# Converting float64 weights 1024 values a partition at a time instead of twice 512

## The chip, the cores and the metric

One core of a Trainium2 chip runs the whole program. The metric is the device time in microseconds (us); lower is better. Engines are named as in the profile: PE (matrix engine), PEld (its weight loads), DVE (VectorE), ACT (ScalarE), POOL (GpSimd), SP (the queue that issues the DMA transfers).

## The reference

Three stages on 4608 tokens (8 batches of 576): pooled attention in float32, then two feed-forward layers. All weights of the layers are float64.

```python
def _attn_ref(q, k, v):                    # (8, 8, 576, 64), pool = 8
    k_p = k.reshape(B, H, Sp, pool, D).mean(axis=3)
    v_p = v.reshape(B, H, Sp, pool, D).mean(axis=3)
    scores = scale * np.matmul(q, k_p.transpose(0, 1, 3, 2))
    ...
    return np.matmul(attn, v_p).astype(np.float32)

def _moe_ref(x, w1, w2, w3, w_out):        # 512 -> 1024 -> 512
    a = x @ w1
    b = x @ w2
    h = a * b @ w3
    return (h @ w_out).astype(np.float32)

def _moe2_ref(x, w_in, w_out):             # 512 -> 2048 -> 512
    h = x @ w_in
    g = np.maximum(h, 0.0) + np.log1p(np.exp(-np.abs(h)))
    return (g @ w_out).astype(np.float32)
```

## The kernel before

**Conversion jobs.** The chip's engines compute in float32, so the kernel turns the float64 weights into float32 itself, from their bits. A job takes 1024 float64 values a partition (1 MB in all). `load_raw` loads them in two transfers of 512 values a partition, each into a buffer of its own (`raw`, four buffers). `convert_steps` then works in steps, each for both halves one after the other: ACT scales the high word (L100); DVE clamps (L103) and shifts it (L105); DVE puts in the sign (L108); DVE puts in the low word's bits (L111). For w12, wi and wo2 the result is split further into two terms of reduced precision for the fast matmul mode: ACT rounds it (L115) and DVE takes the remainder (L118). The intermediate tiles `y` of such a job come from the shared tag `t2k` (eight buffers). The steps of a job are a generator; `bg(n)` runs n steps of the queued jobs at a given place of the program, so conversions are scattered between other work. When a job ends, `load_ahead` issues the next load, so that two jobs' data are loaded or under way.

**Stages.** There are 36 jobs. First come twelve for the two matrices whose product W = w3 @ w_out replaces two of the reference's matmuls (names `wo`, `w3_`; their tiles are `wgh`/`wgl`); PE multiplies them (`W_mm`, tiles `Wp`) while the attention of the first token groups runs in slots between. `W_split` (ACT, then DVE, tiles `Wh`, `Wl`) ends that stage, and the first layer's matmuls (`ab`) follow. Eight jobs give the groups of w1 and w2 (`w_0` to `w_7`), three of them before W's split and five after it. From then on nine blocks of 512 tokens go through the first layer: a step multiplies x with a group of w1 (`ab`, even groups) and one of w2 (odd groups), DVE multiplies the two (`g`), ACT and DVE split the result (`gh`, `gl`), and a step later PE multiplies it with W (`x2p`). Two PSUM banks take turns for `ab`: the one that DVE's `g` reads is written again by the next step's second product. Attention slots lie between until all token groups are done. During the last two blocks the sixteen jobs of the second layer begin (`wi0` to `wi7`, and eight for wo2, tiles `w2h`, `w2l`): four are queued behind the last attention slot, 2 + 3 + 2 in the last block, and five for the first steps of the second layer. The second layer then runs 9 x 16 steps (`h`, softplus on ACT and DVE, `o`), the `o` product three steps behind `h`.

Between the layers x2 goes through DRAM; `x2_load` brings a block back, and `x2_split` splits its four parts.

**Order.** The program is written in order by hand; each engine runs its instructions in that order, and waits where one isn't ready. SP issues the transfers in that order too, and waits for the buffer of each.

Of the kernel before, what the change touches and what calls it, by code (L numbers as in the profile page):

```python
# [15 lines left out]
P = 128  # L16
# [32 lines left out]
def pooled_attention_two_ffn(ctx: ExitStack, tc: tile.TileContext, qT_d, kT_d, v_d, w12_d, w3T_d, wo_d, wi_d, wo2_d, out):  # L49
# [23 lines left out]
    def t2k(name, dt=F32):  # L73
        return main.tile([P, 512], dt, tag="t2k", name=name, bufs=8)
# [12 lines left out]
    def load_raw(src, name):  # L87

        raw = main.tile([P, 512, 2], I32, tag="raw", name=f"raw_{name}", bufs=4)
        nc.sync.dma_start(raw.rearrange("p n t -> p (n t)"), src.bitcast(I32))  # L90
        return raw

    def convert_steps(raws, dsts, name):


        both = range(len(raws))
        y = [t2k(f"y_{name}_{i}") if isinstance(dsts[i], tuple) else dsts[i] for i in both]
        yi = [t.bitcast(I32) for t in y]
        for i in both:
            nc.scalar.activation(y[i], raws[i][:, :, 1].bitcast(F32), AF.Abs, scale=HI_SCALE)  # L100
        yield
        for i in both:
            nc.vector.tensor_scalar(y[i], y[i], HI_MIN, HI_MAX, op0=ALU.max, op1=ALU.min)  # L103
        for i in both:
            nc.vector.tensor_scalar(yi[i], yi[i], 3, None, op0=ALU.logical_shift_left)  # L105
        yield
        for i in both:
            nc.vector.scalar_tensor_tensor(yi[i], raws[i][:, :, 1], -0x80000000, yi[i], op0=ALU.bitwise_and, op1=ALU.bitwise_or)  # L108
        yield
        for i in both:  # L110
            nc.vector.scalar_tensor_tensor(yi[i], raws[i][:, :, 0], 29, yi[i], op0=ALU.logical_shift_right, op1=ALU.bitwise_or)  # L111
        yield
        if isinstance(dsts[0], tuple):
            for i in both:
                nc.scalar.activation(dsts[i][0], y[i], AF.Copy)  # L115
            yield
            for i in both:
                nc.vector.tensor_sub(dsts[i][1], y[i], dsts[i][0].bitcast(F32))  # L118

# [7 lines left out]
    def load_ahead():  # L127
        while jobs and len(loaded) < 2:
            name, srcs, dst = jobs.pop(0)
            loaded.append((name, [load_raw(s_, f"{name}_{i}") for i, s_ in enumerate(srcs)], dst))  # L130

    def next_job():
        load_ahead()
        name, raws, dst = loaded[0]
        yield from convert_steps(raws, dst(), name)
        loaded.pop(0)
        converted.add(name)
        load_ahead()
# [11 lines left out]
    def add_group(src, slot, name, into):  # L150


        def dst():
            hi = main.tile([P, KD, 256], F32R, tag=f"wgh{slot}", name=f"{name}h")
            lo = main.tile([P, KD, 256], F32R, tag=f"wgl{slot}", name=f"{name}l")
            into[slot] = hi, lo
            return [tuple(w[:, 2 * i:2 * i + 2, :].rearrange("p k f -> p (k f)") for w in (hi, lo)) for i in range(2)]

        add_job(name, [src[:, 2 * i:2 * i + 2, :] for i in range(2)], dst)
# [8 lines left out]
    def load_q(n):  # L168
        t = ap_.tile([P, 4, 256], F32, tag="q", name=f"q{n}", bufs=3)
        nc.sync.dma_start(t, qT_d[n])  # L170
        q_t[n] = t
# [128 lines left out]
    for g in range(NG):  # L300
        o = STEPS_FIRST if g < 4 else STEPS_DENSE if g < 8 or g >= NG - 4 else STEPS
        if o[3] < o[4]:
            at(begin[g] + o[4], lambda g=g: x_split(g))
        at(begin[g], lambda g=g: scores(g))
        at(begin[g] + o[0], lambda g=g: softmax(g))
        at(begin[g] + o[1], lambda g=g: normalize(g))
        at(begin[g] + o[2], lambda g=g: p_transpose(g))
        at(begin[g] + o[3], lambda g=g: pv(g))
        if o[3] == o[4]:
            at(begin[g] + o[3], lambda g=g: x_split(g))  # L310
        if g % 2 == 1 and g // 2 + 3 < NG // 2:
            at(begin[g] + 1, lambda g=g: load_q(g // 2 + 3))
# [20 lines left out]
    with tc.manual_schedule():  # L333
# [13 lines left out]
        def wo_dst(kk):  # L347
# [5 lines left out]
            return [wo_hl[kk], wo_hl[kk + 1]]  # L353

        def w3_dst(kk):
            if kk % 2 == 0:
                w3_hl["t"] = tiles_of(4 + kk // 2, 512)
            w3_hl[kk] = w3_hl["t"][kk % 2]
            return [w3_hl[kk][:, 0, :], w3_hl[kk][:, 1, :]]

        for kk in range(K1):
            if kk % 2 == 0:
                add_job(f"wo{kk}", [wo_d[(kk + i) * P:(kk + i + 1) * P, :] for i in range(2)], lambda kk=kk: wo_dst(kk))
            add_job(f"w3_{kk}", [w3T_d[kk * P:(kk + 1) * P, 512 * i:512 * i + 512] for i in range(2)], lambda kk=kk: w3_dst(kk))
# [27 lines left out]
        for n in range(3):  # L392
# [4 lines left out]
            if n:  # L397
# [99 lines left out]
        def x2_load(j):  # L497
            raw = fin.tile([P, KD, TB], F32, tag="x2raw", name=f"x2r{j}")
            nc.sync.dma_start(raw, x2d[j])
            x2h[j, "raw"] = raw  # L500

        def x2_split(j, kk):
# [3 lines left out]
            split(x2h[j][:, kk, :], x2l[j][:, kk, :], x2h[j, "raw"][:, kk, :])  # L506
# [10 lines left out]
        x2_load(0)  # L517
        for i in range(K1):
            p1_step(NB - 1, i, [slot_3, slot_2, slot_2])
            if 1 <= i < 5:  # L520
                x2_split(0, i - 1)
            if i % 2 == 1 and i < 7:
# [64 lines left out]
        for n in range(len(seq) + LAG):  # L587
            if n < len(seq):
# [5 lines left out]
                if j + 1 < NB:  # L594
                    if f == 1:
                        x2_load(j + 1)
                    if f in (7, 9, 11, 13):
                        x2_split(j + 1, (f - 7) // 2)
# [55 lines left out]
```

## Time and profile before

| | |
|---|---|
| median of 3 runs | 1596.8 us (1596.24 to 1597.06) |
| profiled execution: its own time | 1598.61 us |
| profiled execution: span, first to last instruction | 1596.8 us |
| mean granted clock of PE | 0.996 of full speed |
| busy share of the span: PE, PEld, DVE, ACT | 97%, 79%, 53%, 50% |
| instructions: DVE, ACT | 1452, 1813 |
| DMA, mean | 60 GB/s |

The busy share is an average over stages. A time in a view counts from the span's start. PE's busy time holds matmuls whose ends are modelled. "Idle before" is the engine's idle time just ahead of an instruction, with what ended it.

### The profile page before, as it was taken

To read this page: it belongs to the slowest core of one execution; us is meant where nothing else is said; L and a number is where in the kernel's file an instruction comes from. 1 tells how busy PE (TensorE), PEld (TensorE's weight loads), DVE (VectorE), ACT (ScalarE), POOL (GpSimd) and SP (SyncE) were. 2 spreads that over 40 slices of the span, in tenths; PEclk is the share of its full clock that TensorE was granted. 3 is DMA by queue.
4 is the path that set the end of the run, shared out by engine and by line. 5 is a ranking of instruction groups with operands and counts; after the bars stand their busy time and mean duration, and the time that the engine had idled before them with its cause. 6 is when DMAs were issued, how large, how long until landed. Compare 5 with 4: busy or idle time off the path is not lost.

```text
span 1596.8 us, 19269 instructions
## 1 busy us (share of the span) xinstructions
PE 1556.2 (97%) x7424; PEld 1254.9 (79%) x7424; DVE 853.7 (53%) x1452; ACT 799.7 (50%) x1813; POOL 1.7 (0%) x8
## 2 busy tenths in 40 slices
PE   4898999999999999999999999999999999999999
PEld 2457888888888888878878888888888888888887
DVE  6896534243433434327878755555555555555554
ACT  3555433343434343334467665556565565565554
POOL 0000000000000000000000000000000000000000
PEclk9999999999999999999999999999999999999999
DMA  8652212021212111204341101000000001010000
GB/s 275 212 185 76 90 46 66 25 76 37 77 36 63 52 62 29 79 1 158 132 132 54 53 1 53 1 27 27 27 27 27 27 1 53 1 53 1 7 20 27
DMA packets 32011, 95.61 MB, mean 60 GB/s; under 512 B 3632, under 2 KB 3632, under 8 KB 30768
## 3 DMA queue, kind: packets, MB, share of 16 engines
q1 hardware_dynamic: 31920, 94.39, 18.1%
q8 instruction: 58, 0.95, 0.3%
q14 instruction: 33, 0.27, 0.1%
HBM read 75.50 MB, written 18.87 MB: 59 GB/s over the span
## 4 chain that ended last, share of the span: by engine, by line
PE 84%; DVE 8%; ACT 4%; DMA 2%; issue 1%; SPq 0%; ACTq 0%; DVEq 0%
PE ab L82 8%; PE o L573 7%; PE ab L84 7%; PE ab L83 7%; PE o L575 7%; PE o L574 7%; PE h L82 7%; PE h L83 7%; PE h L84 7%; PE x2p L82 4%; PE x2p L84 4%; PE x2p L83 4%; PE sc L213 2%; PE pv L262 2%; PE pTp L244 2%; DMA raw_w<-in_w3T_dram 1%
## 5 line engine op out<-in xcount | busy, mean ns | idle before, releaser
L79 DVE TENSOR_TENSOR g2l<-d,g2h 128x512 fp32r<-128x512 f32 x144 | 99.6, 692 | 328.9 <-ACT g2h L78 328.9
L573 PE MATMUL o<-w2h,g2h 128*128 128x512 f32 x576 | 224.8, 390 | 1.8 <-DVE x2s L445 1.7
L575 PE MATMUL o<-w2h,g2l 128*128 128x512 f32 x576 | 224.2, 389 | 0.0
L574 PE MATMUL o<-w2l,g2h 128*128 128x512 f32 x576 | 224.2, 389 | 0.0
L543 ACT ACTIVATE e<-h 128x512 f32<-128x512 f32 x144 | 85.8, 596 | 270.2 <-PE h L84 270.2
L78 ACT ACTIVATE gh<-g 128x512 fp32r<-128x512 f32 x72 | 45.5, 633 | 179.1 <-DVE g L428 179.1
L573 PEld LDWEIGHTS o<-w2h,g2h 128*128 128x128 f32 x576 | 108.1, 188 | 26.6 <-DVE x2s L445 2.1
L575 PEld LDWEIGHTS o<-w2h,g2l 128*128 128x128 f32 x576 | 108.1, 188 | 23.0 <-DVE g2l L79 0.4
L574 PEld LDWEIGHTS o<-w2l,g2h 128*128 128x128 f32 x576 | 108.1, 188 | 21.8
L82 PE MATMUL x2p<-gh,Wh 128*128 128x512 f32 x288 | 116.1, 403 | 0.0
L84 PE MATMUL x2p<-gh,Wl 128*128 128x512 f32 x288 | 112.6, 391 | 0.0
L83 PE MATMUL x2p<-gl,Wh 128*128 128x512 f32 x288 | 112.3, 390 | 0.0
L227 ACT ACTIVATE pr<-sc,mx 128x72 f32<-128x72 f32 x288 | 87.7, 331 | 48.8 <-DVE mx L225 48.7
L428 DVE TENSOR_TENSOR g<-a,ab 128x512 f32<-128x512 f32 x72 | 49.4, 686 | 108.1 <-PE ab L84 107.0
L553 DVE TENSOR_TENSOR d<-d,l 128x512 f32<-128x512 f32 x144 | 99.7, 692 | 5.0
L552 DVE SCALAR_TENSOR_TENSOR d<-h,d 128x512 f32<-128x512 f32 x144 | 99.6, 692 | 5.0
L551 DVE SCALAR_TENSOR_TENSOR d<-u,e 128x512 f32<-128x512 f32 x144 | 98.7, 685 | 1.0 <-ACT u L546 1.0
L79 DVE TENSOR_TENSOR xl<-pv,xh 128x512 fp32r<-128x512 f32 x36 | 24.8, 690 | 135.5 <-ACT xh L78 135.5
L546 ACT ACTIVATE u<-e 128x512 f32<-128x512 f32 x144 | 91.0, 632 | 10.1 <-DVE d L551 5.7
L548 ACT ACTIVATE l<-u 128x512 f32<-128x512 f32 x144 | 91.1, 633 | 4.7
L544 ACT ACTIVATE e<-e 128x512 f32<-128x512 f32 x144 | 91.0, 632 | 4.6
L78 ACT ACTIVATE g2h<-d 128x512 fp32r<-128x512 f32 x144 | 88.6, 615 | 3.5 <-DVE d L553 2.8
(207 smaller groups left out, 3209.7 us busy)
## 6 DMA issues: line engine op xcount, KB each, us to landing
raw_wo<-in_wo_dram SPq DMA_DIRECT2D x24, 512.0 KB
kv<-in_kT_dram SPq DMA_DIRECT2D x32, 288.0 KB
q<-in_qT_dram SPq DMA_DIRECT2D x18, 512.0 KB
kv<-in_v_dram SPq DMA_DIRECT2D x32, 288.0 KB
x2d<-x2s SPq DMA_DIRECT2D x36, 256.0 KB
x2r<-x2d SPq DMA_DIRECT2D x9, 1024.0 KB
out_dram<-os SPq DMA_DIRECT2D x36, 256.0 KB
raw_w<-in_w3T_dram SPq DMA_DIRECT2D x16, 512.0 KB
```

The lines of the kernel that those rows point to most:

```text
L78: nc.scalar.activation(hi, src, AF.Copy)
L79: nc.vector.tensor_sub(lo, src, hi.bitcast(F32))
L82: nc.tensor.matmul(ps, whi, xhi, start=first, stop=False)
L83: nc.tensor.matmul(ps, whi, xlo, start=False, stop=False)
L84: nc.tensor.matmul(ps, wlo, xhi, start=False, stop=last)
L548: nc.scalar.activation(ln, u, AF.Ln)
L551: nc.vector.scalar_tensor_tensor(d, u, 1.0, e, op0=ALU.subtract, op1=ALU.subtract)
L552: nc.vector.scalar_tensor_tensor(d, ps, 0.0, d, op0=ALU.max, op1=ALU.subtract)
L553: nc.vector.tensor_add(d, d, ln)
L573: nc.tensor.matmul(oacc[j][t], hi[:, s_], wh, start=f == 0, stop=False)
L574: nc.tensor.matmul(oacc[j][t], hi[:, s_], wl, start=False, stop=False)
L575: nc.tensor.matmul(oacc[j][t], lo[:, s_], wh, start=False, stop=f == K2 - 1)
```

## The change

A job's data lie in one buffer of 1024 values a partition (`raw`, two buffers) and each step of a job is one instruction over 1024 values. Weights whose rows lie in one piece in DRAM are loaded in one transfer (w3, w12, wi); wo and wo2, whose two halves are different rows, in two. `y` gets buffers of its own (`y4k`, two of 4 KB a partition). For w12 and wi the two steps of the further split work on 1024 values as well; for wo2 they stay two instructions of 512. To make room, `t2k` has six buffers instead of eight and `q` two instead of three (so the third q tile is loaded later), and `x2_load` brings half a block at a time into a buffer of half the size, the second half behind the second split.

```diff
@@ -71,7 +71,7 @@
         return at_p.tile([P, 512], F32, tag="at", name=name)
 
     def t2k(name, dt=F32):
-        return main.tile([P, 512], dt, tag="t2k", name=name, bufs=8)
+        return main.tile([P, 512], dt, tag="t2k", name=name, bufs=6)
 
     def split(hi, lo, src):
 
@@ -84,39 +84,37 @@
         nc.tensor.matmul(ps, wlo, xhi, start=False, stop=last)
 
 
-    def load_raw(src, name):
-
-        raw = main.tile([P, 512, 2], I32, tag="raw", name=f"raw_{name}", bufs=4)
-        nc.sync.dma_start(raw.rearrange("p n t -> p (n t)"), src.bitcast(I32))
+    def load_raw(srcs, name):
+
+        raw = main.tile([P, 1024, 2], I32, tag="raw", name=f"raw_{name}", bufs=2)
+        n = 1024 // len(srcs)
+        for i, src in enumerate(srcs):
+            nc.sync.dma_start(raw[:, n * i:n * i + n, :].rearrange("p n t -> p (n t)"), src.bitcast(I32))
         return raw
 
-    def convert_steps(raws, dsts, name):
-
-
-        both = range(len(raws))
-        y = [t2k(f"y_{name}_{i}") if isinstance(dsts[i], tuple) else dsts[i] for i in both]
-        yi = [t.bitcast(I32) for t in y]
-        for i in both:
-            nc.scalar.activation(y[i], raws[i][:, :, 1].bitcast(F32), AF.Abs, scale=HI_SCALE)
+    def convert_steps(raw, dst, name):
+
+
+        split_ = isinstance(dst, list)
+        y = main.tile([P, 1024], F32, tag="y4k", name=f"y_{name}", bufs=2) if split_ else dst
+        yi = y.bitcast(I32)
+        nc.scalar.activation(y, raw[:, :, 1].bitcast(F32), AF.Abs, scale=HI_SCALE)
         yield
-        for i in both:
-            nc.vector.tensor_scalar(y[i], y[i], HI_MIN, HI_MAX, op0=ALU.max, op1=ALU.min)
-        for i in both:
-            nc.vector.tensor_scalar(yi[i], yi[i], 3, None, op0=ALU.logical_shift_left)
+        nc.vector.tensor_scalar(y, y, HI_MIN, HI_MAX, op0=ALU.max, op1=ALU.min)
+        nc.vector.tensor_scalar(yi, yi, 3, None, op0=ALU.logical_shift_left)
         yield
-        for i in both:
-            nc.vector.scalar_tensor_tensor(yi[i], raws[i][:, :, 1], -0x80000000, yi[i], op0=ALU.bitwise_and, op1=ALU.bitwise_or)
+        nc.vector.scalar_tensor_tensor(yi, raw[:, :, 1], -0x80000000, yi, op0=ALU.bitwise_and, op1=ALU.bitwise_or)
         yield
-        for i in both:
-            nc.vector.scalar_tensor_tensor(yi[i], raws[i][:, :, 0], 29, yi[i], op0=ALU.logical_shift_right, op1=ALU.bitwise_or)
+        nc.vector.scalar_tensor_tensor(yi, raw[:, :, 0], 29, yi, op0=ALU.logical_shift_right, op1=ALU.bitwise_or)
         yield
-        if isinstance(dsts[0], tuple):
-            for i in both:
-                nc.scalar.activation(dsts[i][0], y[i], AF.Copy)
+        if split_:
+            n = 1024 // len(dst)
+            parts = [y[:, n * i:n * i + n] for i in range(len(dst))]
+            for part, (hi, lo) in zip(parts, dst):
+                nc.scalar.activation(hi, part, AF.Copy)
             yield
-            for i in both:
-                nc.vector.tensor_sub(dsts[i][1], y[i], dsts[i][0].bitcast(F32))
-
+            for part, (hi, lo) in zip(parts, dst):
+                nc.vector.tensor_sub(lo, part, hi.bitcast(F32))
 
 
     jobs, loaded, converted = [], [], set()
@@ -127,12 +125,12 @@
     def load_ahead():
         while jobs and len(loaded) < 2:
             name, srcs, dst = jobs.pop(0)
-            loaded.append((name, [load_raw(s_, f"{name}_{i}") for i, s_ in enumerate(srcs)], dst))
+            loaded.append((name, load_raw(srcs, name), dst))
 
     def next_job():
         load_ahead()
-        name, raws, dst = loaded[0]
-        yield from convert_steps(raws, dst(), name)
+        name, raw, dst = loaded[0]
+        yield from convert_steps(raw, dst(), name)
         loaded.pop(0)
         converted.add(name)
         load_ahead()
@@ -154,9 +152,9 @@
             hi = main.tile([P, KD, 256], F32R, tag=f"wgh{slot}", name=f"{name}h")
             lo = main.tile([P, KD, 256], F32R, tag=f"wgl{slot}", name=f"{name}l")
             into[slot] = hi, lo
-            return [tuple(w[:, 2 * i:2 * i + 2, :].rearrange("p k f -> p (k f)") for w in (hi, lo)) for i in range(2)]
-
-        add_job(name, [src[:, 2 * i:2 * i + 2, :] for i in range(2)], dst)
+            return [tuple(w.rearrange("p k f -> p (k f)") for w in (hi, lo))]
+
+        add_job(name, [src.rearrange("p k f -> p (k f)")], dst)
 
 
     ident = main.tile([P, P], F32, tag="ident", name="ident")
@@ -166,7 +164,7 @@
     q_t, kT_t, vb_t, kv_raw = {}, {}, {}, {}
 
     def load_q(n):
-        t = ap_.tile([P, 4, 256], F32, tag="q", name=f"q{n}", bufs=3)
+        t = ap_.tile([P, 4, 256], F32, tag="q", name=f"q{n}", bufs=2)
         nc.sync.dma_start(t, qT_d[n])
         q_t[n] = t
 
@@ -308,8 +306,8 @@
         at(begin[g] + o[3], lambda g=g: pv(g))
         if o[3] == o[4]:
             at(begin[g] + o[3], lambda g=g: x_split(g))
-        if g % 2 == 1 and g // 2 + 3 < NG // 2:
-            at(begin[g] + 1, lambda g=g: load_q(g // 2 + 3))
+        if g % 2 == 1 and g // 2 + 2 < NG // 2:
+            at(begin[g] + 1, lambda g=g: load_q(g // 2 + 2))
 
 
     first, last = {}, {}
@@ -350,18 +348,18 @@
             t = wo_hl["t"][kk // 2 % 2]
             for i in range(2):
                 wo_hl[kk + i] = t[:, i, :]
-            return [wo_hl[kk], wo_hl[kk + 1]]
+            return t.rearrange("p i f -> p (i f)")
 
         def w3_dst(kk):
             if kk % 2 == 0:
                 w3_hl["t"] = tiles_of(4 + kk // 2, 512)
             w3_hl[kk] = w3_hl["t"][kk % 2]
-            return [w3_hl[kk][:, 0, :], w3_hl[kk][:, 1, :]]
+            return w3_hl[kk].rearrange("p i f -> p (i f)")
 
         for kk in range(K1):
             if kk % 2 == 0:
                 add_job(f"wo{kk}", [wo_d[(kk + i) * P:(kk + i + 1) * P, :] for i in range(2)], lambda kk=kk: wo_dst(kk))
-            add_job(f"w3_{kk}", [w3T_d[kk * P:(kk + 1) * P, 512 * i:512 * i + 512] for i in range(2)], lambda kk=kk: w3_dst(kk))
+            add_job(f"w3_{kk}", [w3T_d[kk * P:(kk + 1) * P, :]], lambda kk=kk: w3_dst(kk))
         for s_ in range(8):
             add_group(w12_d[s_], s_, f"w12_{s_}", wgroups)
 
@@ -394,7 +392,7 @@
             for _ in range(3 if n < 2 else 2):
                 kv_step()
             W_ready(2)
-            if n:
+            if n == 1:
                 load_q(n)
         for n in range(START):
             att_slot()
@@ -494,16 +492,16 @@
 
         x2h, x2l = {}, {}
 
-        def x2_load(j):
-            raw = fin.tile([P, KD, TB], F32, tag="x2raw", name=f"x2r{j}")
-            nc.sync.dma_start(raw, x2d[j])
+        def x2_load(j, half):
+            raw = fin.tile([P, 2, TB], F32, tag="x2raw", name=f"x2r{j}_{half}")
+            nc.sync.dma_start(raw, x2d[j][:, 2 * half:2 * half + 2, :])
             x2h[j, "raw"] = raw
 
         def x2_split(j, kk):
             if kk == 0:
                 x2h[j] = main.tile([P, KD, TB], F32R, tag="xh", name=f"x2h{j}", bufs=2)
                 x2l[j] = main.tile([P, KD, TB], F32R, tag="xl", name=f"x2l{j}", bufs=2)
-            split(x2h[j][:, kk, :], x2l[j][:, kk, :], x2h[j, "raw"][:, kk, :])
+            split(x2h[j][:, kk, :], x2l[j][:, kk, :], x2h[j, "raw"][:, kk % 2, :])
 
         def slot_2():
             bg(2)
@@ -514,11 +512,13 @@
         background += [next_job() for _ in range(4)]
         for i in range(i7, K1):
             p1_step(NB - 2, i, [slot_2] * 3)
-        x2_load(0)
+        x2_load(0, 0)
         for i in range(K1):
             p1_step(NB - 1, i, [slot_3, slot_2, slot_2])
             if 1 <= i < 5:
                 x2_split(0, i - 1)
+            if i == 2:
+                x2_load(0, 1)
             if i % 2 == 1 and i < 7:
                 background += [next_job() for _ in range(3 if i == 3 else 2)]
         background += [next_job() for _ in range(5)]
@@ -592,10 +592,10 @@
                 if n == 1:
                     x2_mm(NB - 1, K1 - 1)
                 if j + 1 < NB:
-                    if f == 1:
-                        x2_load(j + 1)
-                    if f in (7, 9, 11, 13):
-                        x2_split(j + 1, (f - 7) // 2)
+                    if f in (1, 8):
+                        x2_load(j + 1, f // 8)
+                    if f in (5, 7, 11, 13):
+                        x2_split(j + 1, {5: 0, 7: 1, 11: 2, 13: 3}[f])
             else:
                 h_split()
             if n >= LAG:
```

Lines of the changed kernel: L101, L103, L104, L106, L108 are the conversion's five steps, L114 and L117 the two of the further split.

Where the rows of DVE stand at the end of the stage that makes W, first before. `y_w_2` is the intermediate tile of the third group of w1 and w2, `w_2l` its remainder, `Wl` that of W's split:

```order
L108 SCALAR_TENSOR_TENSOR y_w_2_0_658<-raw_w_2_0_628,y_w_2_0_658 128x512
L108 SCALAR_TENSOR_TENSOR y_w_2_1_659<-raw_w_2_1_630,y_w_2_1_659 128x512
L111 SCALAR_TENSOR_TENSOR y_w_2_0_658<-raw_w_2_0_628,y_w_2_0_658 128x512
L111 SCALAR_TENSOR_TENSOR y_w_2_1_659<-raw_w_2_1_630,y_w_2_1_659 128x512
L118 TENSOR_TENSOR w_2l<-y_w_2_0_658,w_2h 128x512
L118 TENSOR_TENSOR w_2l<-y_w_2_1_659,w_2h 128x512
L79 TENSOR_TENSOR Wl_697<-Wp_97,Wh_696 128x512
L79 TENSOR_TENSOR Wl_701<-Wp_98,Wh_700 128x512
```

The same place now:

```order
L103 TENSOR_SCALAR y_w_2_552<-y_w_2_552 128x1024
L104 TENSOR_SCALAR y_w_2_552<-y_w_2_552 128x1024
L106 SCALAR_TENSOR_TENSOR y_w_2_552<-raw_w_2_534,y_w_2_552 128x1024
L108 SCALAR_TENSOR_TENSOR y_w_2_552<-raw_w_2_534,y_w_2_552 128x1024
L117 TENSOR_TENSOR w_2l<-y_w_2_552,w_2h 128x1024
L79 TENSOR_TENSOR Wl_581<-Wp_97,Wh_580 128x512
L79 TENSOR_TENSOR Wl_585<-Wp_98,Wh_584 128x512
```

Each pair became one row over 1024 values; the sequence is the same, and nothing stands between L108 (low word) and L117 (remainder), nor between L117 and W's split. The job before it, `w_1`, stands the same way.

Where the rows of DVE stand near the end of the first layer, in the last block's step 6, first before. `y_wo_8` belongs to a pair of wo2's row blocks, `y_wi` to a group of wi; `g_6` and `gl_6` are the step's product and its split:

```order
L111 SCALAR_TENSOR_TENSOR y_wo_8_0_6183<-raw_wo_8_0_6117,y_wo_8_0_6183 128x512
L111 SCALAR_TENSOR_TENSOR y_wo_8_1_6184<-raw_wo_8_1_6119,y_wo_8_1_6184 128x512
L118 TENSOR_TENSOR w2l_6180<-y_wo_8_0_6183,w2h_6179 128x512
L118 TENSOR_TENSOR w2l_6182<-y_wo_8_1_6184,w2h_6181 128x512
L103 TENSOR_SCALAR y_wi_0_6232<-y_wi_0_6232 128x512
L103 TENSOR_SCALAR y_wi_1_6233<-y_wi_1_6233 128x512
L105 TENSOR_SCALAR y_wi_0_6232<-y_wi_0_6232 128x512
L105 TENSOR_SCALAR y_wi_1_6233<-y_wi_1_6233 128x512
L428 TENSOR_TENSOR g_6_6253<-a_6_6220,ab_6_1_6240 128x512
L79 TENSOR_TENSOR gl_6_6256<-g_6_6253,gh_6_6255 128x512
L108 SCALAR_TENSOR_TENSOR y_wi_0_6232<-raw_wi_0_6175,y_wi_0_6232 128x512
L108 SCALAR_TENSOR_TENSOR y_wi_1_6233<-raw_wi_1_6177,y_wi_1_6233 128x512
```

The same place now:

```order
L108 SCALAR_TENSOR_TENSOR y_wo_8_5954<-raw_wo_8_5899,y_wo_8_5954 128x1024
L117 TENSOR_TENSOR w2l_5951<-y_wo_8_5954,w2h_5950 128x512
L117 TENSOR_TENSOR w2l_5953<-y_wo_8_5954,w2h_5952 128x512
L103 TENSOR_SCALAR y_wi_5995<-y_wi_5995 128x1024
L104 TENSOR_SCALAR y_wi_5995<-y_wi_5995 128x1024
L426 TENSOR_TENSOR g_6_6012<-a_6_5985,ab_6_1_5999 128x512
L79 TENSOR_TENSOR gl_6_6015<-g_6_6012,gh_6_6014 128x512
L106 SCALAR_TENSOR_TENSOR y_wi_5995<-raw_wi_5948,y_wi_5995 128x1024
L108 SCALAR_TENSOR_TENSOR y_wi_5995<-raw_wi_5948,y_wi_5995 128x1024
```

`g_6` stands at the same place between the same steps. Ahead of it the pairs of L111, L103 and L105 are one row each, and the two rows of the remainder stay.

## Rows read from the trace of the kernel before

**Rows 1.** The table by stretches: us, busy us by engine, clock, DMA share, GB/s.

```profile
0.00:105.60 105.60, 78.23 (x257) 38.90 (x257) 85.96 (x171) 45.51 (x133) 1.73 (x8) 0.94 0.75 239
105.60:180.00 74.40, 69.19 (x386) 56.24 (x387) 51.96 (x103) 39.54 (x123) 0.00 (x0) 1.00 0.27 85
180.00:680.00 500.00, 500.00 (x2734) 410.52 (x2733) 189.07 (x339) 187.09 (x642) 0.00 (x0) 1.00 0.18 55
680.00:726.00 46.00, 43.60 (x243) 35.27 (x242) 12.88 (x27) 16.88 (x60) 0.00 (x0) 1.00 0.01 1
726.00:821.00 95.00, 93.33 (x412) 76.96 (x411) 80.16 (x150) 50.65 (x88) 0.00 (x0) 1.00 0.44 147
821.00:1596.80 775.80, 771.88 (x3400) 636.97 (x3398) 433.62 (x665) 460.04 (x772) 0.00 (x0) 1.00 0.08 29
```

**Rows 2.** Waits of PE: waiter, releaser, us in total, times, longest.

```profile
PE o L573 <- DVE x2s L445: 1.7, 1, 1.7
```

**Rows 3.** The chain of waits, 0 to 106 us: start, us, what.

```profile
1.18 4.66 DMA raw_wo<-in_wo_dram
...
12.97 9.53 DMA raw_w<-in_w3T_dram
...
35.30 5.95 DMA raw_w<-in_w3T_dram
...
66.38 4.97 DMA raw_w<-in_w3T_dram
...
78.89 8.36 DMA raw_w<-in_w_dram
...
104.94 1.20 DVE Wl L79 x2
```

**Rows 4.** Timeline behind the landing of w3_1: start, us, what, idle before.

```profile
22.52 0.66 ACT L100 ACTIVATE wgl<-raw_w 128x512 f32<-128x512 f32 x1 [1.83 <-DMA raw_w<-in_w3T_dram]
...
23.22 0.43 DVE L103 TENSOR_SCALAR wgl<-wgl 128x512 f32<-128x512 f32 x1 [2.06 <-ACT wgl L100]
23.56 0.76 DVE L105 TENSOR_SCALAR wgl<-wgl 128x512 int32<-128x512 int32 x2
```

**Rows 5.** Groups by shape: count, busy us, mean ns, idle before.

```profile
L552 DVE SCALAR_TENSOR_TENSOR d<-h,d 128x512 f32<-128x512 f32 x144 | 99.6, 692 | 5.0
...
L201 DVE TENSOR_REDUCE vb<-kv 72x128 f32<-72x1024 f32 x32 | 38.5, 1206 | 0.0
...
L193 ACT ACTIVATE kT<-ks 64x72 f32<-64x72 f32 x64 | 16.7, 261 | 39.6 <-DVE ks L190 39.2
...
L115 ACT ACTIVATE w2h<-y_wo 128x512 fp32r<-128x512 f32 x16 | 9.8, 633 | 25.5 <-DVE y_wo L111 25.5
...
L100 ACT ACTIVATE wgh<-raw_w 128x512 f32<-128x512 f32 x8 | 5.1, 664 | 5.0 <-DMA raw_w<-in_w3T_dram 5.0
```

**Rows 6.** Timeline of DVE, 755 to 809 us.

```profile
758.61 0.99 DVE L103 TENSOR_SCALAR y_wi<-y_wi 128x512 f32<-128x512 f32 x2 [1.86 <-ACT y_wi L100]
...
774.93 1.00 DVE L103 TENSOR_SCALAR y_wi<-y_wi 128x512 f32<-128x512 f32 x2 [0.54 <-ACT y_wi L100]
...
792.59 1.28 DVE L111 SCALAR_TENSOR_TENSOR y_wo<-raw_wo,y_wo 128x512 int32<-128x512 int32 x2
793.98 1.29 DVE L118 TENSOR_TENSOR w2l<-y_wo,w2h 128x512 fp32r<-128x512 f32 x2
...
796.73 0.68 DVE L428 TENSOR_TENSOR g<-a,ab 128x512 f32<-128x512 f32 x1
...
807.84 0.69 DVE L79 TENSOR_TENSOR gl<-g,gh 128x512 fp32r<-128x512 f32 x1 [0.70 <-ACT gh L78]
```

**Rows 7.** Timeline of PE, 797.9 to 809.2 us.

```profile
797.98 0.39 PE L82 MATMUL ab<-xh,w_7h 128*128 128x512 f32 x1
...
809.09 0.39 PE L83 MATMUL x2p<-gl,Wh 128*128 128x512 f32 x1
```

**Rows 8.** Timeline of SP, the DMA issues, 0 to 36 us.

```profile
1.65 0.90 SPq L90 DMA_DIRECT2D raw_w<-in_w3T_dram  x2
```

## The prediction

> **What bounds the kernel now.** I read the table by stretches first [rows 1]. The matrix engine (PE) has no idle time between 180 and 680 us, and 3.9 us after 821 us, with the drain at the end. What it loses besides lies in the start (105.6 - 78.2 = 27.4 us, most of it the fill), from there to 180 us (5.2 us), and in two short places (2.4 and 1.7 us). At full clock almost everything else is bound by matmuls, of which the change touches none. So only stretches in which weights are converted can move: the start, with twelve conversion jobs for the product W and three for the first w12 groups, and 726 to 821 us, with eleven jobs (4 + 2 + 3 + 2 are queued there). In both VectorE (DVE) is the busy engine: 86.0 of 105.6 us and 80.2 of 95.0 us [rows 1].
>
> The chain of waits [rows 3] then says what ended last in the start. Five times it goes through a weight load that had to land, and it ends with W's split on DVE at 104.94 us, queued behind the conversions of the first three groups. In 726 to 821 us the view to read is DVE's timeline beside PE's [rows 6, 7]: DVE is late against PE. g of step 6 ends at 796.73 + 0.68 = 797.41 us, and PE starts the next product, which writes the bank that g read (there are two), at 797.98 us, 0.57 us later. gl of step 7 ends at 808.53 us and is read by the matmul at 809.09 us, 0.56 us later. Another 0.6 us of lag there is a stall on PE. Soon after, PE already waits 1.7 us for DVE's copy [rows 2].
>
> **The change, part by part.**
>
> *Fewer, longer DVE instructions.* A job had 8 (or 10) DVE instructions of 512 columns and now has 4 to 6, most of 1024. A pair takes 1.28 us [rows 6], a reduction over 1024 elements 1.21 us [rows 5]: about 0.07 us saved for each pair, 0.3 us a job. But the pairs also hid a dependency. In a pair the second half runs while the first half's result arrives, and the next instruction starts 0.60 us after the last (1.28 - 0.68). Where an instruction reads what the one straight before it wrote, it starts 0.692 us plus 0.035 us of idle time after it (5.0 us over 144) [rows 5], so 0.13 us later. The changed order has L103 and L104 always adjacent and the next two steps mostly so: about 2.4 such pairs a job, 0.3 us paid. I take the net as zero. Its bounds are all saved and nothing paid, -0.3 us for each of 26 jobs (-4.5 us in the start, -3.3 us later), and +0.1 us a job.
>
> The Trainium skill says otherwise (VectorE: DVE Perf Modes, "The DRAIN you can't avoid"): an instruction drains whether or not the next one waits for it, so waits cost nothing and the count alone matters. By that rule the sum below would be nearly 8 us lower. The trace disagrees: 0.60 against 0.73 us from start to start.
>
> *The handover between ScalarE (ACT) and DVE is no longer split.* This is the main cost. ACT took 0.261 us for 72 columns and 0.633 us for 512 [rows 5], 0.85 ns a column; an estimate for 1024 columns is 0.633 + 0.43 = 1.06 us for L115 and 0.664 + 0.43 = 1.10 us for L100. (Bounds: 0.66 us if the columns cost nothing, 1.33 us if nothing is saved against two; I take the value from the slope.) Three places follow.
> First, behind a landing: now the last half lands, ACT takes its half, DVE its half of L103 while the first half is done, and L105 starts 23.56 - 22.52 = 1.04 us after ACT did [rows 4]. Then it is 1.10 + 0.04 + 0.69 + 0.04 = 1.87 us, +0.8 us for each of the five landings on the chain: +4.1 us.
> Second, from L111 to L118 in split jobs: L118 starts 0.11 us after L111's end (793.98 against 793.87) [rows 6], since ACT rounds the first half during the second half of L111. Then ACT starts when L111 is over: 1.06 + 0.05 = 1.11 us, so +1.0 us of idle DVE unless something stands between. For second-layer output weights L118 stays in halves, but the next job's L103 waits for ACT to finish both and its own L100, which comes to the same.
> Third, in two start jobs whose data lies ready (w3_0 and w3_4), ACT's 1.10 instead of 0.66 us precedes DVE: +0.8 us together.
>
> *Loads.* One issue instead of two for w3, w12 and wi saves 0.45 us of queue time (0.90 for two) [rows 8] before the last byte is asked for: -0.45 us on four of the five landings, -1.8 us. The first half of a buffer is no longer freed 0.6 us ahead of the second; these I leave as the margin of this term (-1.8 to +1.5 us).
>
> *q in two buffers.* The third q tile's 0.5 MB leaves the start, ahead of a w3 load in SP's queue. At 239 GB/s for a share of 0.75, so 319 GB/s at a full one [rows 1], that is 1.6 us: -1.6 us (0 if that load was not late). Later each q load still waits for the same scores as now and is wanted three groups later.
>
> *Costed at nothing.* Six t2k buffers instead of eight: the two y tiles of a job leave them, and a buffer comes round after three steps; without that cover a step would wait for a store of 0.25 MB. x2 in halves: the second half is issued behind split 1 and wanted one step (8 us) later; it may hold ACT a microsecond at 773 us, where it now waits for PE, so I give up DVE's idle 0.54 us there.
>
> **The sum.** Start: +4.1 + 0.8, then +2.0 (w_1 and w_2, L118 straight behind L111, ahead of W's split), -1.8 - 1.6 = +3.5 us; bounds 0 and 9. 726 to 821 us: seven of the eleven jobs have L118 straight behind L111, 7 x 1.0 = 7.0; three of the others have g and gl between, but gh waits on ACT behind the longer L115, +0.3 each, 0.9; DVE's idle 1.86 us at 758 us and 0.54 us at 775 us [rows 6] take up 2.4; PE's slack 0.6. That is +4.9 us; bounds 0 and 9. After 821 us other work stands between the steps and PE has three steps of lead: 0. The wait of 1.7 us stays, since copy and matmul move together.
> Together +8.4 us on the profiled execution's 1598.6 us (span 1596.8 us and 1.8 us around it), 1607.0 us; the median of the runs is 1596.8 us, so 1605.2 us there. I say 1605.
>
> **The rivals.** What a measurement of this kernel can tell from no change is 0.2%, 3.2 us.
> *Only one stretch pays.* The other is covered: in the start by the loads sharing a saturated queue (a landing asked for later may arrive no later), or later by a slower PE giving DVE time. +1 to +4.5 us, 1598 to 1601. For it: 9.53 us for one load [rows 3] is far above 5 us, so the queue sets it.
> *No difference.* The loads' gains (3.4 us) and the count's savings meet the handovers: 1594 to 1598.
> *Faster.* The time goes with the number of instructions: DVE saves its full 0.3 us in 26 jobs and the loads give 3.4 us, with the handovers covered: -7.8 - 3.4 = -11.2 us, 1585.6, at its best, and 1592 if half of it lies on the path. It decides if ACT's long instruction takes hardly more than 0.7 us. DVE's shares of 0.81 and 0.84 speak for it, ACT's slope against it.
> The Trainium skill has both sides in one section (Perfetto Trace Analysis, "Optimizing Scalar/DVE Operations"): larger operations help a saturated engine, and smaller ones finish sooner where an engine that isn't saturated makes others wait. Here the share is high, but the waits are handovers, so I side with the second half.
> *Worse.* PE idles long enough in the start for its granted clock (0.94 there [rows 1]) to fall for another stretch of W's matmuls, or the second x2 load is late: 1611 and above.
>
> **How the numbers follow.** Forecast (both stretches pay, 1601 to 1611) 0.60; one stretch 0.16; none 0.11; faster 0.08; worse 0.05. The range leaves out the faster case, the worse one and a little of "none": 1597 to 1611; the forecast's own range is 1601 to 1610. Slower by over 0.2% (above 1600.0): 0.60 + 0.05 + half of 0.16 = 0.73; within: 0.19; faster: 0.08.
>
> **What would show it.** In the profile after: ACT's L100 and L115 with 1024 columns near 1.1 us; DVE idle about 1 us before L117 (now L118) in some ten jobs; L103 to L104 start to start near 0.73 us; PE's first ab matmul near 109 us instead of 105.6; stalls of PE between 795 and 825 us (after shifting) of 5 to 7 us instead of 1.7. Wrong if ab starts at or before 106 us, if the dependent spacing equals the independent one, or if PE shows no new wait before 825 us.

## The result and the profile after

The changed kernel takes 1610.6 us (median of 4 runs, 1609.8 to 1611.4), the kernel before in the same comparison 1596.9 us: ratio 1.008, 95% interval 1.006 to 1.0099. It is slower, by 13.7 us where 8.4 us were forecast; 1610.6 us lies inside the range stated (1597 to 1611) by 0.4 us only, and just above the forecast's own (1601 to 1610). The profiled execution took 1609.98 us with a span of 1608.2 us, 11.4 us more than before's; this pair is taken apart here.

The table by stretches, cut where PE starts the same work as in [rows 1]:

```profile
0.00:107.90 107.90, 72.84 (x257) 36.24 (x257) 84.40 (x108) 43.50 (x116) 1.74 (x8) 0.98 0.67 230
...
125.80:133.00 7.20, 6.67 (x24) 5.15 (x26) 4.13 (x5) 1.23 (x3) 0.00 (x0) 0.55 0.26 74
...
731.40:830.00 98.60, 93.86 (x410) 76.22 (x409) 77.89 (x97) 47.20 (x71) 0.00 (x0) 1.00 0.42 142
```

DVE has 63 instructions fewer in the start and 53 fewer in the late stretch, and is busy for less time in both (84.4 for 86.0 us, 77.9 for 80.2 us), while both stretches became longer. So the loss isn't more work on DVE, it is waiting. In the 500 us of the middle PE is busy for 500.00 us in either kernel.

PE's timeline, its first matmul after the stalls that the text goes by (start, us, what, idle before):

```profile
107.87 0.50 PE L82 MATMUL ab<-xh,w_0h 128*128 128x512 f32 x1 [1.79 <-DVE Wl L79]
126.33 1.89 PE L242 MATMUL pTp<-ident,pr 128*72 128x128 f32 x8 [3.13 <-DVE pr L233]
164.65 1.04 PE L242 MATMUL pTp<-ident,pr 128*72 128x128 f32 x8 [1.69 <-DVE pr L233]
806.42 0.50 PE L82 MATMUL ab<-xh,w_7h 128*128 128x512 f32 x1 [2.18 <-DVE g L426]
829.84 0.50 PE L573 MATMUL o<-w2h,g2h 128*128 128x512 f32 x1 [1.84 <-DVE x2s L443]
901.34 0.50 PE L573 MATMUL o<-w2h,g2h 128*128 128x512 f32 x1 [1.16 <-ACT g2h L78]
```

Before, the first of these started at 105.60 us [rows 1] and the others that answer to them so, with no stall at the step of 806 us [rows 7]:

```profile
123.75 1.04 PE L244 MATMUL pTp<-ident,pr 128*72 128x128 f32 x8 [2.80 <-DVE pr L235]
159.28 1.04 PE L244 MATMUL pTp<-ident,pr 128*72 128x128 f32 x8 [1.69 <-DVE pr L235]
...
820.21 0.50 PE L573 MATMUL o<-w2h,g2h 128*128 128x512 f32 x1 [1.67 <-DVE x2s L445]
```

So the lag is 2.3 us when the first layer starts, 2.6 at the transposes near 126 us, 5.4 at those near 165 us, the same at 705 us, 9.6 at 829.84 us, and 11.4 at the end.

DVE's timeline at the second group of w12, `w_1`, one job from its clamp to the next job's:

```profile
94.66 0.69 DVE L103 TENSOR_SCALAR y_w<-y_w 128x1024 f32<-128x1024 f32 x1
95.39 0.69 DVE L104 TENSOR_SCALAR y_w<-y_w 128x1024 int32<-128x1024 int32 x1
96.12 1.23 DVE L106 SCALAR_TENSOR_TENSOR y_w<-raw_w,y_w 128x1024 int32<-128x1024 int32 x1
97.38 1.23 DVE L108 SCALAR_TENSOR_TENSOR y_w<-raw_w,y_w 128x1024 int32<-128x1024 int32 x1
99.73 1.23 DVE L117 TENSOR_TENSOR w_1l<-y_w,w_1h 128x1024 fp32r<-128x1024 f32 x1 [1.12 <-ACT w_1h L114]
100.87 0.69 DVE L103 TENSOR_SCALAR y_w<-y_w 128x1024 f32<-128x1024 f32 x1
```

The same job before:

```profile
94.32 0.75 DVE L103 TENSOR_SCALAR y_w<-y_w 128x512 f32<-128x512 f32 x2
...
96.87 1.28 DVE L111 SCALAR_TENSOR_TENSOR y_w<-raw_w,y_w 128x512 int32<-128x512 int32 x2
98.24 1.29 DVE L118 TENSOR_TENSOR w_1l<-y_w,w_1h 128x512 fp32r<-128x512 f32 x2
99.46 0.96 DVE L103 TENSOR_SCALAR y_w<-y_w 128x512 f32<-128x512 f32 x2
```

It took 99.46 - 94.32 = 5.14 us; now 100.87 - 94.66 = 6.21 us. The idle 1.12 us ahead of L117 is the handover: ACT rounds only when all of L108 is done. In the late stretch the view of line L117 sums that idle time (releaser: us, times), 6.5 us in eight jobs:

```profile
  ACT w2h L114: 2.9, 4
  ACT wi2h L114: 1.1, 1
  ACT wi4h L114: 1.1, 1
  ACT wi0h L114: 1.1, 1
  ACT wi5h L114: 0.3, 1
```

### The profile page after: what moved, and what is told of

The parts are those of the page before. It is cut to its first block, busy times and chain, and to the rows that moved or that the text cites. A ratio compares the mean times of both kernels' runs of the same rounds, so it can differ in the third digit from the quotient of the medians.

```text
span 1608.2 us, 18973 instructions
## 1 busy us (share of the span) xinstructions
PE 1555.3 (97%) x7424; PEld 1253.9 (78%) x7424; DVE 849.2 (53%) x1292; ACT 792.2 (49%) x1761; POOL 1.7 (0%) x8
## 4 chain that ended last, share of the span: by engine, by line
PE 81%; DVE 11%; ACT 5%; issue 1%; DMA 1%; SPq 0%; ACTq 0%; DVEq 0%
PE o L573 7%; PE o L575 7%; PE o L574 7%; PE ab L82 7%; PE h L84 7%; PE h L83 7%; PE h L82 7%; PE ab L84 7%; PE ab L83 7%; PE x2p L82 3%; PE x2p L84 3%; PE x2p L83 3%; PE sc L211 2%; PE pv L260 2%; PE pTp L242 2%
## 5 line engine op out<-in xcount | busy, mean ns | idle before, releaser
L573 PEld LDWEIGHTS o<-w2h,g2h 128*128 128x128 f32 x576 | 108.2, 188 | 27.8 <-DVE x2s L443 2.3
```

The source lines that it names most:

```text
L573: nc.tensor.matmul(oacc[j][t], hi[:, s_], wh, start=f == 0, stop=False)
```

## The experiments

Names of lines are those of the changed kernel, though each kernel's rows have its own. Fences give the core of each edit against the changed kernel. The sums of "one job" are for `w_1`, as above.

**Which part of the change.** One kernel keeps buffers, loads, q and x2 of the change, but computes in pairs of 512 (one step is shown, the others likewise):

```diff
-        nc.scalar.activation(y, raw[:, :, 1].bitcast(F32), AF.Abs, scale=HI_SCALE)
+        for c in (slice(0, 512), slice(512, 1024)):
+            nc.scalar.activation(y[:, c], raw[:, c, 1].bitcast(F32), AF.Abs, scale=HI_SCALE)
...
```

> The changed kernel's buffers, loads, q and x2 handling, with the conversion's instructions over 512 values again, in pairs as before. Theory 1 (the lost pairs: ACT hands over to DVE only when all 1024 values are done, and DVE's dependent instructions stand alone): the time falls back to 1595 to 1599 us; DVE's first-layer lag is gone, so PE waits under 0.5 us at the last block's step 7 and under 2 us for the copy of x2. Rival (the loss is in the loads and buffers: a job waits for a whole landing, a buffer is freed as a whole, x2 comes in halves): at least 1605 us, PE's first ab matmul still at 107 us or later.

Measured 1599.1 us, ratio 0.9994 (0.9985 to 1.0004): no loss. One job is back at 5.13 us.

The opposite, everything of the change but with two transfers for each load (`add_job(name, [src[:, 2 * i:2 * i + 2, :] ... for i in range(2)], dst)`):

> The changed kernel with every job's data loaded in two transfers of 512 values a partition, compute over 1024. Theory 1: within 2 us of the changed kernel's 1610.6 us, 0 to 2 us slower, since only 0.45 us of queue time per load comes back. Rival (merged transfers delay the landing): 1600 us or less.

1612.9 us, ratio 1.0089 (1.0073 to 1.0104), which can't be told from the change. Loads and buffers carry neither a loss nor a gain that can be seen in the times.

**Which stretch.** Pairs of 512 as above, but 1024 wide in only the sixteen second-layer jobs, or in only the first twenty jobs:

```diff
+    def wide(name):
+        return name.startswith(("wo2_", "wi"))      # the other kernel: not ...
```

> 1024 values an instruction only in the second layer's sixteen jobs, pairs of 512 in the first twenty. Theory 1: the late loss alone, read from the traces as 4.2 us up to the copy of x2 and about 1 us at 901 us, so 1600 to 1603 us, with PE waiting some 2 us at step 7 of the last block; no wait of PE at the changed kernel's sizes before 130 us. Rival (all loss comes from the start and the clock stretch behind it): 1597 to 1598 us.

> 1024 values an instruction only in the first twenty jobs, pairs of 512 in the second layer's sixteen. Theory 1: 2.3 us at PE's first ab matmul, 0.3 us at the wait behind it, and what PE's clock gives away: in the changed kernel's profile it was granted half for 6.8 us of matmuls near 126 us, about 3 us. So 1599.5 to 1604 us; with halves late, PE's waits in the last block as before. If the stretch at half clock comes from the longer waits of PE, it is in this kernel's profile and not in that of the kernel wide only late. Rival (late jobs carry it all): 1597 to 1598 us.

1604.9 us, ratio 1.0039 (1.0026 to 1.0052), and 1604.1 us, 1.0033 (1.002 to 1.0045). Both stretches pay, and the two add up to 0.7%, against 0.8% together. Both times lie at or just above the upper end of what was expected; the kernel before took 1598.9 us in that comparison.

**Which engine's width.** ACT's instructions 1024 wide and DVE's in halves; then DVE's conversion steps 1024 wide, ACT's and L117 in halves:

> Only ACT's scale (L101) and, for w12 and wi, its rounding (L114) are over 1024 values; every DVE step is in two halves. Theory 1 (the handover between ACT and DVE is no longer split): most of the loss is back, since DVE's first half waits for all of ACT's instruction and ACT's rounding for both halves of L108; the eight wo2 jobs keep their split rounding, so somewhat less than the changed kernel: 1602 to 1609 us, ratio 1.003 to 1.007, DVE idle near 1.0 us ahead of L117 of w12 and wi. Theory 2 (what costs is DVE's own rows: a wait on the instruction straight before it): DVE keeps its pairs, so no loss: 1596 to 1600 us, ratio 0.999 to 1.001.

> DVE's conversion steps (L103, L104, L106, L108) are over 1024 values; ACT's instructions and the remainder (L117) are in halves. Theory 1 (handover): L103 now waits for two ACT halves (1.33 us instead of 0.66), and ACT's first rounding for the whole of L108, so DVE idles 0.7 us ahead of L117 instead of 1.1: two thirds of the loss or a little more, 1602 to 1607 us, ratio 1.003 to 1.006. Theory 2 (dependent neighbours on DVE): the whole loss, 1607 to 1612 us, ratio 1.006 to 1.009.

1607.0 us, ratio 1.0048 (1.0034 to 1.0061), and 1610.9 us, 1.0068 (1.0055 to 1.0081). Either side alone breaks the handover. With ACT wide, DVE idles ahead of the remainder as long as in the changed kernel:

```profile
101.15 1.29 DVE L124 TENSOR_TENSOR w_1l<-y_w,w_1h 128x512 fp32r<-128x512 f32 x2 [1.18 <-ACT w_1h L119]
```

With DVE wide, the wait is shorter there, but a second one stands at the next job's clamp, which needs both of ACT's halves:

```profile
98.64 1.29 DVE L127 TENSOR_TENSOR w_1l<-y_w,w_1h 128x512 fp32r<-128x512 f32 x2 [0.76 <-ACT w_1h L124]
100.29 0.69 DVE L108 TENSOR_SCALAR y_w<-y_w 128x1024 f32<-128x1024 f32 x1 [0.36 <-ACT y_w L105]
```

The first excludes that DVE's own rows are the whole cause (theory 2 had 1.000). The second came out above what theory 1 had for it and inside theory 2's range, so the handover wasn't the whole of it either.

**DVE's own rows.** Halves everywhere, but dependent neighbours:

```diff
+        for c in cuts:
+            nc.vector.tensor_scalar(y[:, c], y[:, c], HI_MIN, HI_MAX, ...)
+            nc.vector.tensor_scalar(yi[:, c], yi[:, c], 3, None, ...)
+        yield
+        for c in cuts:
+            nc.vector.scalar_tensor_tensor(yi[:, c], raw[:, c, 1], -0x80000000, yi[:, c], ...)
+            nc.vector.scalar_tensor_tensor(yi[:, c], raw[:, c, 0], 29, yi[:, c], ...)
+            yield
```

> All instructions in halves of 512, but on DVE L103 and L104 of a half, and L106 and L108 of a half, stand one behind the other, so that each second one reads what the one straight before it wrote (four such neighbours a job). Theory 1 (handover, which stays split here): no more than what the neighbours' 0.13 us add on DVE, 0.5 us a job, of which part lies on the path: 1597 to 1602 us, ratio 1.000 to 1.002. Theory 2 (dependent neighbours carry the loss): 1603 to 1610 us, ratio 1.004 to 1.008. A rule by which such a wait is free gives 1.000, with L103 to L104 0.60 us from start to start instead of 0.73.

1606.9 us, ratio 1.0045 (1.0032 to 1.0058). Theory 1 missed: the handover stays split, and nothing was done to the number of instructions or to their length. The DVE timeline shows what it is:

```profile
96.66 0.42 DVE L107 TENSOR_SCALAR y_w<-y_w 128x512 f32<-128x512 f32 x1
97.11 0.43 DVE L108 TENSOR_SCALAR y_w<-y_w 128x512 int32<-128x512 int32 x1
97.46 0.42 DVE L107 TENSOR_SCALAR y_w<-y_w 128x512 f32<-128x512 f32 x1
...
98.25 0.68 DVE L111 SCALAR_TENSOR_TENSOR y_w<-raw_w,y_w 128x512 int32<-128x512 int32 x1
98.97 0.69 DVE L112 SCALAR_TENSOR_TENSOR y_w<-raw_w,y_w 128x512 int32<-128x512 int32 x1
99.58 0.69 DVE L111 SCALAR_TENSOR_TENSOR y_w<-raw_w,y_w 128x512 int32<-128x512 int32 x1
...
102.31 0.42 DVE L107 TENSOR_SCALAR y_w<-y_w 128x512 f32<-128x512 f32 x1
```

An instruction starts 0.35 us after its neighbour where it doesn't read it (97.11 to 97.46) and 0.45 us where it does (96.66 to 97.11); 0.61 and 0.72 us for the longer ones. One job takes 102.31 - 96.66 = 5.65 us, 0.5 us more than in pairs; its four such neighbours make 0.42 of it. The Trainium skill (VectorE: DVE Perf Modes, "The DRAIN you can't avoid") says of its own measurement that a wait between neighbours costs nothing extra. The trace disagrees, by 0.10 to 0.11 us each time.

The count, by four instructions of 256 in place of each two of 512 on DVE, none reading its neighbour:

> Handovers as before, ACT in halves of 512, but DVE's four conversion steps in quarters of 256, no instruction reading what the one straight before it wrote: eight more instructions a job. If each instruction costs the 0.07 us that two merged into one saved, DVE takes 0.5 to 0.6 us more a job; with the exchange that the kernel with dependent neighbours showed (26 jobs x 0.5 us gave 7 us) that is 1604 to 1609 us, ratio 1.003 to 1.006. If the count costs nothing: 1597 to 1601 us, ratio 0.999 to 1.001.

1609.9 us, ratio 1.0071 (1.0056 to 1.0085), a little above what was expected. A step of four starts the next one after 96.68 - 95.87 = 0.81 us, where two of 512 took 0.67 and one of 1024 takes 0.61 (in the changed kernel 846.77 to 847.38 us; 0.73 with a dependent neighbour):

```profile
95.87 0.89 DVE L108 TENSOR_SCALAR y_w<-y_w 128x256 f32<-128x256 f32 x4
96.68 0.89 DVE L110 TENSOR_SCALAR y_w<-y_w 128x256 int32<-128x256 int32 x4
...
101.61 0.49 DVE L108 TENSOR_SCALAR y_w<-y_w 128x256 f32<-128x256 f32 x2
```

One job takes 101.61 - 95.87 = 5.74 us, 0.6 us more than in pairs. So both prices are real. Halves at the handovers alone (L101, L103, L108, L114, L117), and 1024 values for L104 and L106, sets them against each other:

> Halves only at the handovers: L101, L103, L108, L114 and L117 are in halves, L104 and L106 over 1024 values. Theory 1 (handover): the loss is gone, 1597 to 1602 us, ratio 0.999 to 1.002; DVE's own account is three neighbours of 0.12 us against two merged pairs of 0.07 us, 0.2 us a job, at the same exchange up to 3 us. Theory 2 (long instructions or neighbours by themselves): at least half of the loss stays, ratio 1.004 to 1.008.

1601.4 us, ratio 1.002 (1.0011 to 1.0029): three quarters of the loss are gone with the handovers split. One job takes 98.44 - 93.06 = 5.38 us, 0.24 us more than in pairs, which is what DVE's own account gave:

```profile
93.06 0.75 DVE L107 TENSOR_SCALAR y_w<-y_w 128x512 f32<-128x512 f32 x2
...
98.44 0.97 DVE L107 TENSOR_SCALAR y_w<-y_w 128x512 f32<-128x512 f32 x2
```

**The handover by itself.** The late jobs stay 1024 wide and the others in halves, as in the kernel with the ratio 1.0039, and the idle time is filled: ACT scales the next job's data ahead of this job's L108, and DVE clamps and shifts them between L114 and L117.

```diff
         nc.vector.scalar_tensor_tensor(yi, raw[:, :, 1], ...)      # L106
+        scale_high(following)
         yield
         nc.vector.scalar_tensor_tensor(yi, raw[:, :, 0], 29, ...)  # L108
         ...
+        clamp_shift(following)
+        yield
         nc.vector.tensor_sub(lo, part, hi.bitcast(F32))            # L117
```

> Second-layer jobs over 1024 values as in the kernel that widens only these (ratio 1.0039), but the next job's scale on ACT goes ahead of this job's L108, and its clamp and shift on DVE stand between this job's rounding (L114) and its remainder (L117). Theory 1 (DVE idles for want of work at the handover): the loss of the late stretch goes, 1595 to 1600 us, ratio 0.998 to 1.001, no stall of PE near 806 us beyond 1 us. Theory 2 (length or dependency of DVE's instructions): the same instructions are still there, ratio 1.003 to 1.005.

1606.1 us, ratio 1.0037 (1.0024 to 1.005): no gain, and a miss by its number. But the late stretch has one stall, and it is another one: PE waits for ACT, which stands at a scale whose data have not landed, with `a` of the current step behind it (PE's row, then ACT's):

```profile
762.25 0.79 PE L82 MATMUL ab<-xh,w_2h 128*128 128x512 f32 x1 [7.70 <-ACT a L480]
...
760.59 1.12 ACT L139 ACTIVATE y_wi<-raw_wi 128x1024 f32<-128x1024 f32 x1 [11.41 <-DMA raw_wi<-in_wi_dram]
```

Drawing work ahead on an engine that runs in order had put a load into the path. The stall has a second price: from 762 to 766 us the granted clock was 0.50, the lower level (1.2 GHz). So the load was issued three steps earlier, the scale went one step later, and the first wi job isn't drawn ahead:

```diff
         yield
+        if following and following[0] != "wi0": scale_high(following)
         nc.vector.scalar_tensor_tensor(yi, raw[:, :, 0], 29, ...)  # L108
+        loaded.pop(0)
+        load_ahead()
```

> As the kernel that fills the handover, with its two flaws mended: the next job's load is issued as soon as L108 has read the buffer (three steps earlier), its scale on ACT stands one step later, and the first wi job, whose data came last, isn't drawn ahead. Theory 1 (DVE idles at the handover): the late loss (ratio 1.0039 with these jobs wide) goes, 1595 to 1601 us, ratio 0.998 to 1.001. Theory 2 (DVE's own rows, length and neighbours): 1602 to 1606 us, ratio 1.002 to 1.005. A stall of PE that ACT ends, as the 7.7 us one, would leave it undecided.

1596.6 us, ratio 0.9987 (0.9978 to 0.9996): the late loss is gone. Its interval lies just below 1; the median's 0.13% is less than the 0.2% that the prediction takes as the least that can be told. The idle time of DVE ahead of the remainder is down to 0.7 us, and of PE's late waits that had grown one of 0.8 us is left:

```profile
  ACT w2h L171: 0.7, 1
...
PE ab L82 <- DVE g L487: 0.8, 1, 0.8
```

Since the loads were changed as well, the control has the earlier load and no filling:

> The control for the kernel with the filled handover and the earlier load: second-layer jobs over 1024 values, the next load issued as soon as L108 has read the buffer, but nothing filled in; DVE's order is that of the kernel that widens only these jobs. Theory 1 (the handover's idle DVE, which the filling took away): the late loss stays, ratio 1.002 to 1.005, 1601 to 1606 us, with DVE idle 0.7 to 1.1 us ahead of L117 again. Theory 2 (the loads, which came too late with two buffers): the loss is gone by the earlier load alone, ratio 0.998 to 1.001.

1605.4 us, ratio 1.0045 (1.003 to 1.006). The idle time is back (6.5 us in the same eight places), and so are PE's late waits:

```profile
  ACT w2h L169: 2.9, 4
...
PE ab L82 <- DVE g L484: 2.6, 2, 2.2
...
PE o L631 <- ACT g2h L78: 1.1, 1, 1.1
```

The same instructions of the same length, with the handover filled or not, make the whole difference in the late stretch. That is shown. For the start it is shown only that width costs there (1.0033), and that splitting the handovers in all jobs gives most of it back.

## Why the prediction was right, and where its sizes were off

**The handover** was the main cause, as forecast, and its sizes hold. Behind the landing of w3_1 L104 starts 24.38 - 22.48 = 1.90 us after ACT did (forecast 1.87, before 1.04 [rows 4]). L101 took a little longer than estimated (1.14 for 1.10 us), and L114 1.06 us as estimated:

```profile
22.48 1.14 ACT L101 ACTIVATE wgl<-raw_w 128x1024 f32<-128x1024 f32 x1 [2.69 <-DMA raw_w<-in_w3T_dram]
24.38 0.69 DVE L104 TENSOR_SCALAR wgl<-wgl 128x1024 int32<-128x1024 int32 x1
98.64 1.06 ACT L114 ACTIVATE w_1h<-y_w 128x1024 fp32r<-128x1024 f32 x1 [4.01 <-DVE y_w L108]
```

**The start** came to +2.3 us in the profile, forecast +3.5, and here the nearness is partly luck. The chain of waits has the last landing of a w3 weight in the changed kernel and in the one in halves so:

```profile
66.87 4.89 DMA raw_w<-in_w3T_dram
...
66.17 4.99 DMA raw_w<-in_w3T_dram
```

It ends at 71.76 us in the changed kernel, 0.4 us later than the 66.38 + 4.97 = 71.35 us of before [rows 3]; four times 0.82 and 0.8, less three times 0.45 and 1.6, had made 1.1. But neither term shows at its size. Halves, which has the loads and the two q buffers without the long handover, ends it at 71.16 us: 0.2 us gained where 3.0 were forecast, and 0.6 us then paid for the length where 4.1 were forecast. From there on the changed kernel's path has no landing of a w12 weight any more, where before had one of 8.36 us [rows 3]: the fifth +0.8 wasn't paid. At `w_1` the lag is 94.66 - 94.32 = 0.34 us; `w_1` adds 1.07 us and `w_2` 0.86, forecast 1.0 each.

Nor can one pair of profiles size the start. Five of the kernels above share the code of the start with halves (itself, late jobs alone wide, both filled ones, the earlier load); in their profiles that landing ends at 70.3 to 71.6 us, and PE's first ab starts at 104.8 to 108.2 us. Halves, then late jobs alone wide:

```profile
104.93 0.50 PE L82 MATMUL ab<-xh,w_0h 128*128 128x512 f32 x1
...
108.23 0.50 PE L82 MATMUL ab<-xh,w_0h 128*128 128x512 f32 x1 [1.15 <-DVE Wl L79]
```

That the start pays rests on the times (1.0033), not on these 2.3 us.

**726 to 821 us** came to 9.63 - 5.4 = +4.2 us, forecast +4.9. There are eight waits ahead of L117, not seven, and the four of wo2 are 0.7 us, since ACT's first half comes after 0.62 us; 6.5 us in all against 7.0. No run sizes the smaller terms (+0.9, -2.4, -0.6) one by one. The stalls between 806 and 830 us are 2.18 + 0.23 + 1.84 = 4.25 us, below the 5 to 7 named as the sign.

**DVE's own account at zero** was nearly right. In the start, where all of a job's steps stand together, L103 to L108 take 97.38 - 94.66 = 2.72 us instead of 96.87 - 94.32 = 2.55, and L117 saves 0.08 (99.73 to 100.87 us, before 98.24 to 99.46): +0.1 us, the upper bound given. Both prices that cancel there were found real, 0.5 us a job costing 0.45% and 0.6 us 0.7%. That also sets aside the rival by which the count decides: fewer instructions do save what it said, and their dependent neighbours take it back. Of the two halves of the section that was named beside it (the Trainium skill, Perfetto Trace Analysis, "Optimizing Scalar/DVE Operations") the runs bear out the second for this change: the smaller instructions let the waiting engine go on sooner.

**After 821 us at zero** was the step that failed, with a small sum: the lag grows from 9.6 us at 830 us to 11.4 at 901.34 us, so 1.8 us. It is the handover again, in the last five jobs: ACT runs in order and stands at each rounding until all of L108 is done, 19.7 us at the five roundings behind 830 us instead of 16.5. At the last one (the changed kernel, then before):

```profile
897.14 1.15 ACT L114 ACTIVATE w2h<-y_wo 128x512 fp32r<-128x512 f32 x2 [5.23 <-DVE y_wo L108]
...
885.67 1.24 ACT L115 ACTIVATE w2h<-y_wo 128x512 fp32r<-128x512 f32 x2 [4.65 <-DVE y_wo L111]
```

Behind it wait the softplus steps of the next products, three steps of lead or not: PE starts the `o` product at 901.34 us after a stall of 1.16 us, at 889.95 us before, which is 1.1 us of the 1.8. In halves, and with only the handovers split, PE has no such stall. Another 0.4 us goes at 886.74 us, where PE's weight load waits for the remainder of wi7, and 0.2 us at 872.71 us, where it waits for `g2l`:

```profile
886.74 0.19 PEld L84 LDWEIGHTS h<-x2h,wi7l 128*128 128x128 f32 x1 [0.56 <-DVE wi7l L117]
```

**The clock** wasn't in the sum. Between 125.8 and 133.0 us the granted clock was 0.55, mostly the lower of the two levels (1.2 GHz), behind the stall of 3.13 us; from one row of transposes to the later one it took 164.65 - 126.33 = 38.32 us instead of 159.28 - 123.75 = 35.53: +2.8 us. The rival called "worse" had named such a stretch, but in W's matmuls. It isn't bound to the width: the kernel in halves, with no loss, has it too, and shorter (its table by stretches):

```profile
123.00:127.00 4.00, 3.92 (x15) 3.28 (x16) 3.68 (x8) 1.19 (x2) 0.00 (x0) 0.57 0.02 4
```

It lost 1.6 us there, as did the kernel that is wide only at the start and the one that is wide only late; the one with the earlier load, whose start is that of halves, lost nothing. So how much of the 2.8 us is the change's stays open.

**The sum.** 2.3 + 0.3 + 2.8 + 4.2 + 1.8 = 11.4 us, all of the difference in span (0.3 is the longer stall at 126 us). Against the profiled execution the forecast was 1607.0, the measured one 1609.98: 3.0 us short. The two terms that had a size came 1.9 us below it, and what stood at nothing came to 4.9, most of it the clock, so the total is nearer than its parts. The other 2.5 us between 1605.2 and 1610.6 come from the step to the median: before's profiled execution lay 1.8 us above the median of its runs, and that of after 0.7 us below. The mean granted clock of every run is on record: 0.993 to 0.996 in the four of the changed kernel, 0.994 to 0.997 in the eleven of the one in halves. How much of the 13.7 us goes with it, and whether the longer waits bring it about, no run shows; the interval leaves 9.6 us at the least for the whole change.

## What to carry to other kernels

Where two engines handed a tile to each other here, two half-size instructions made a pipeline and one full-size instruction a wait of its whole length. Merge them only where other work stands in the gap, or put it there; and when work is drawn ahead on an engine that runs in order, see first that its data have landed. On a busy DVE, count dependent neighbours as well as instructions: interleaving two halves paid here about as much as merging them saved.

## What the runs showed of the hardware

- A DVE instruction that reads its neighbour's result started 0.10 to 0.12 us later than one that doesn't, at 512 columns (0.45 for 0.35, 0.72 for 0.61 us) and at 1024 (1.26 us from L106's start to L108's, 1.14 us from L117's to the clamp's behind it).
- The same 1024 columns in one, two or four instructions on DVE, none reading its neighbour, took 0.61, 0.67 and 0.81 us to the next start: 0.06 to 0.07 us for each instruction more.
- Soon behind PE's stall that ends at 123 to 130 us the granted clock fell in some executions and not in others, whatever the width. From 123 to 135 us its mean was 1.00 in before and with ACT alone wide, DVE alone wide, the handovers split, and the late jobs filled at first or only loaded earlier; 0.86 or 0.87 in the seven other experiments; 0.72 in the changed kernel. The way between the two rows of transposes took 35.5 us in the first group, 37.0 to 37.1 in the second, 38.3 in the last.
